# A tuned attention and mixture-of-experts kernel: each PSUM bank of the late stage becomes a tile of its own, the last expert's products change order, and the vector work is listed anew

## The chip, the cores and the metric

The kernel runs on one core of a Trainium2 chip. The metric is the device time of one execution in microseconds (us); the number given for a kernel is the median of its runs. The kernel before took 471.54 us, the median of three runs that lay between 467.0 and 472.02 us.

## The reference

Two stages follow each other. The first is an attention that adds a pooled part (queries, keys and values averaged over four positions) to a local part (a band of seven keys). The second is a mixture of four experts, each with two matrix products, over 1152 tokens:

```python
def _attn_ref(q, k, v):                      # 2 x 8 heads x 576 x 64
    ...
    return out_up + out_local                # pooled + banded softmax attention

def _moe_ref(x, domain_probs, w1, w2):       # N, D, E, F = 1152, 512, 4, 1024
    p = domain_probs / (domain_probs.sum(-1, keepdims=True) + 1e-09)
    out = np.zeros((N, D), dtype=np.float32)
    for e in range(E):
        h = np.maximum(x @ w1[e], 0.0)
        out += p[:, e:e + 1] * (h @ w2[e])
    return out
```

Inputs and output are float32. The kernel splits each float32 operand into a high and a low part (fp32r) and adds three matrix products (low x high, high x low, high x high).

## The kernel before, in words

**Stages.** The first 186 us do the attention and expert 0, interleaved. What the change touches is the late stage: experts 1, 2 and 3, one after the other, each in the same pattern. `late_expert(e)` writes it down as steps with a name, an engine and the steps they depend on; the table `ORDER` at the top of the file is a list of all step names, and the steps are issued in exactly that order, so it sets the order of the instructions on each engine. A layer under the kernel then puts the waits (semaphores) between engines by looking at which tiles an instruction reads and writes.

**Products.** Both matrix products of an expert are done with seven block products in place of eight, a fast matrix multiplication over 2 x 2 blocks. The names of the seven are `1 5 6 2 7 4 3`.

- The first matrix product: for each of four slices i of the hidden features there are seven steps `p<m><e><i>` (line 1034), 12 matmuls each: 6 for the first 288 tokens, then 6 for the other 288. They accumulate in the PSUM areas X, Y, Z. After a product an area is drained into the SBUF tile H by a step `t11 t12 t22 h21` on ACT (lines 1043, 1045) or `h11 h12 h22` on DVE (line 1047). There are seven drains for each i, 28 per expert, 84 in all. Each reads 576 columns: both 288-token halves in one instruction.
- The second matrix product: for each of the seven, two steps `s<m><e><h>` for the token halves h = 0 and 1 (line 1220), 24 matmuls each. Their operands are units of H that ACT rounds (`ah`, lines 1131 and 1135) and DVE subtracts (`ao`, lines 1140 and 1144), and blocks of w2 that ACT rounds (`bh`) and DVE subtracts (`bo`, line 1086). Units live in a ring of three buffers. Sums of H that some units need are `as` (line 1118).
- Two steps `c1` and `c2` (line 1233, 24 matmuls each) do the middle 128 tokens in the area W; their operands are the steps `th to tr ts tdh tdo` (lines 1191 to 1201).
- The results are drained into the accumulator `acc` by steps `d<e><name><h>.<t>` on DVE (line 1242, 256 columns each), by `dw` for the middle tokens (line 1247), and for two of the seven by a scaled copy on ACT (`dt`, line 1267) and an accumulating DMA from POOL's queue (`dd`, line 1270). The next product into the same area has to come after the drain. In the last expert, `st` steps on SP's queue store `acc` to the output as it is finished.

**PSUM.** There are eight banks of 512 float32 columns. In the late stage they are four tiles of two banks, `T["banks"]`, each [128, 2, 512]; X, Y, Z and W are one such tile each, and the roles rotate (`BANKS`). A token half h is one bank of the pair:

```python
T["banks"] = [ps.tile([P, 2, 512], F32, name=f"ps{i}") for i in range(4)]
...
def bank(n, i=None):
    return T["banks"][pair(n, i)]
```

**Order of the second product.** PE issues s1, s5, s2, s6 (two halves each), c1, s7, c2, s4, s3. Into X go 1, 6, 7, 4; into Z go 5 and 3; into Y goes 2. So `s7` waits for the drain of 6 (`x2`), `s4` for the drain of 7 (`x3`), and `s3` for the drain of 5 (`z1`).

**Other queues.** w1 comes over SP's queue (`wl`) and is summed on DVE (`ws`); one slice per expert is built by DMAs alone, copies from SP (`wm`) and accumulating adds from POOL (`wa`). w2 blocks come by `bl<e><m>.<k>`: k = 0 from SP, k > 0 as accumulating DMAs from POOL, through two buffers, one of which is used by product 6 and then by product 4.

Of the kernel before, what the change touches and what calls it, by code (L numbers as in the profile page):

```python
# [15 lines left out]
P = 128  # L16
# [60 lines left out]
    dt1x10 ao151.1 th1 as16.0 dd1x10 s510 ah120.0 as16.1 bh13 ao120.0 s511 ah121.0 bo13 ao121.0 bl17.1 s210 bo16
    ah160.0 wa2020 as17.0 dt1x11 bl14.1 s211 ah161.0 ao160.0 dd1x11 ao161.0 s610 ah170.0 to1 ao170.0 tr1 s611 ts1
    ah171.0 d1x20.0 wa2062 d1x20.1 bh17 ao171.0 c11 bo17 ah140.0 dt1y0 d1x21.0 bl21.0 d1x21.1 bh14 dd1y0 ao140.0 s710
    tdh1 bo14 tdo1 bl26.0 as13.0 s711 ah141.0 wh20 d1x30.0 d1x30.1 c21 ah130.0 ao141.0 d1x31.0 dt1y1 d1x31.1 wo20 s410  # L80
    dd1y1 bl26.1 ao130.0 wl21 s411 d1z10.0 ah131.0 d1z10.1 d1z11.0 ao131.0 d1z11.1 s310 wl22 dw1 d1x40.0 d1x40.1
    d1x41.0 d1x41.1 s311 d1z20.0 d1z20.1 ws21 p120 d1z21.0 bl26.2 d1z21.1 p520 t1120 wh21 p620 wo21 p220 t1220 t2220
    p720 bh21 ws22 wl23 p121 h1120 wh22 h2220 bo21 p521 t1121 bl25.1 p420 t2221 p621 h2120 p320 t1221 p221 wo22 p721
    h1220 h1121 p122 h2221 ws23 ah210.0 p522 t1122 ah211.0 ao210.0 p421 wh23 ao211.0 p622 h2121 t2222 as25.0 p321
    t1222 ah250.0 p222 bh25 wo23 p722 h1221 wl30 h1122 p123 wm304 h2222 wm305 wm306 bo25 p523 t1123 ao250.0 bl22.0
    p422 t2223 p623 h2122 p322 t1223 wa3042 p723 bh26 wa3052 p223 h2223 bh22 h1222 p423 ah210.1 ah211.1 ao210.1 p323
    bo22 h2123 h1123 bl23.0 s120 ao211.1 as25.1 h1223 ah250.1 s121 ah251.0 ao250.1 wa3023 ah251.1 ao251.0 dt2x10
    ao251.1 th2 as26.0 dd2x10 s520 ah220.0 as26.1 bh23 ao220.0 s521 ah221.0 bo23 ao221.0 bl27.1 s220 bo26 ah260.0
    wa3020 as27.0 dt2x11 bl24.1 s221 ah261.0 ao260.0 dd2x11 ao261.0 s620 ah270.0 to2 ao270.0 tr2 s621 ts2 ah271.0
    d2x20.0 wa3062 d2x20.1 bh27 ao271.0 c12 bo27 ah240.0 dt2y0 d2x21.0 bl31.0 d2x21.1 bh24 dd2y0 ao240.0 s720 tdh2  # L90
    bo24 tdo2 bl36.0 as23.0 s721 ah241.0 wh30 d2x30.0 d2x30.1 c22 ah230.0 ao241.0 d2x31.0 dt2y1 d2x31.1 wo30 s420
    dd2y1 bl36.1 ao230.0 wl31 s421 d2z10.0 ah231.0 d2z10.1 d2z11.0 ao231.0 d2z11.1 s320 wl32 dw2 d2x40.0 d2x40.1
    d2x41.0 d2x41.1 s321 d2z20.0 d2z20.1 ws31 p130 d2z21.0 bl36.2 d2z21.1 p530 t1130 wh31 p630 wo31 p230 t1230 t2230
    p730 bh31 ws32 wl33 p131 h1130 wh32 h2230 bo31 p531 t1131 bl35.1 p430 t2231 p631 h2130 p330 t1231 p231 wo32 p731
    h1230 h1131 p132 h2231 ws33 ah310.0 p532 t1132 ah311.0 ao310.0 p431 wh33 ao311.0 p632 h2131 t2232 as35.0 p331
    t1232 ah350.0 p232 bh35 wo33 p732 h1231 h1132 p133 h2232 bo35 p533 t1133 ao350.0 bl32.0 p432 t2233 p633 h2132 p332
    t1233 p733 bh36 p233 h2233 bh32 h1232 p433 ah310.1 ah311.1 ao310.1 p333 bo32 h2133 h1133 bl33.0 s130 ao311.1
    as35.1 h1233 ah350.1 s131 ah351.0 ao350.1 ah351.1 ao351.0 dt3x10 ao351.1 th3 as36.0 dd3x10 s530 ah320.0 as36.1
    bh33 ao320.0 s531 ah321.0 bo33 ao321.0 bl37.1 s230 bo36 ah360.0 ao360.0 bl34.1 dt3x11 as37.0 s231 ah361.0 dd3x11
    ao361.0 s630 ah370.0 to3 ao370.0 tr3 s631 ts3 ah371.0 d3x20.0 bh37 d3x20.1 bo37 dt3y0 c13 ah340.0 ao371.0 dd3y0  # L100
    bh34 d3x21.0 d3x21.1 s730 tdh3 ao340.0 tdo3 bo34 s731 ah341.0 d3x30.0 d3x30.1 as33.0 c23 dt3y1 st5.0 st6.0 ao341.0
# [1277 lines left out]
```

## Time and profile before

| | us |
|---|---|
| median of three runs | 471.54 |
| their range | 467.0 to 472.02 |
| the profiled execution's own time | 471.17 |
| span of its trace, first to last instruction | 469.2 |
| PE (matmul) busy | 449.8, 96% of the span |
| DVE busy | 332.6, 71% |
| ACT busy | 202.8, 43% |
| POOL busy | 105.2, 22% |

The span is 1.97 us shorter than the profiled execution's own time. The page cuts the span into 40 slices of 11.7 us; in all but the last PE is busy for 70% or more. TensorE's granted clock is half of full speed for three slices near the start and full after that (the mean over the span is 0.963), so the late stage runs at full clock. The chain of work that ended last, followed back from the end, is PE for 85% of the span and DVE for 5%; where it leaves PE, PE was waiting.

### The profile page before, as it was taken

The numbers are of one execution on the slowest core, as the hardware profiler recorded it, in microseconds if no ns is written. First come the engines' busy times: TensorE is split into PE (matmuls) and PEld (weight loads), VectorE is DVE, ScalarE is ACT, GpSimd is POOL, SyncE is SP. The second block draws the span as 40 slices with busy tenths as digits, with TensorE's granted clock in tenths as the row PEclk, the third lists the DMA queues.
The fourth block names the chain that finished last, engine by engine and source line by source line (L and its number), as shares of the span: only waits on it lengthen the run. The fifth ranks groups of instructions, "written<-read, shape, count | busy, mean of one in ns | idle before, by whom it ended". The sixth has DMA issues, their size and how long they took to land.

```text
span 469.2 us, 10113 instructions
## 1 busy us (share of the span) xinstructions
PE 449.8 (96%) x4266; PEld 425.1 (91%) x4266; DVE 332.6 (71%) x555; ACT 202.8 (43%) x343; POOL 105.2 (22%) x126
## 2 busy tenths in 40 slices
...
GB/s 181 227 265 106 121 57 85 110 29 32 37 1 46 3 89 28 154 88 133 70 58 113 131 173 85 8 146 57 84 126 120 143 91 1 45 46 121 59 27 177
DMA packets 68941, 43.10 MB, mean 92 GB/s; under 512 B 27616, under 2 KB 66720, under 8 KB 68896
## 3 DMA queue, kind: packets, MB, share of 16 engines
...
## 4 chain that ended last, share of the span: by engine, by line
PE 85%; DVE 5%; POOL 4%; DMA 2%; issue 2%; ACT 1%; SPq 0%; DVEq 0%; POOLq 0%; ACTq 0%
PE ps L1034 29%; PE ps L1220 26%; PE m03h L778 4%; PE m03o L803 3%; POOL wlo L306 3%; PE m02h L778 3%; PE m01h L778 3%; PE m01o L803 2%; PE m02o L803 2%; PE m00o L803 2%; DVE acc L1242 1%; DMA acc<-in_q_dram 1%; PE m00h L778 1%; PE ps L1233 1%; PE wps L232 1%
## 5 line engine op out<-in xcount | busy, mean ns | idle before, releaser
L1220 PE MATMUL ps<-slot,unit 128*128 128x256 f32 x1008 | 121.2, 281 | 6.3 <-DVE acc L1242 6.2
L1220 PEld LDWEIGHTS ps<-slot,unit 128*128 128x128 f32 x1008 | 119.2, 188 | 8.0 <-ACT slot L1199 4.3
L1034 PE MATMUL ps<-xhi,slot 128*128 128x288 f32 x384 | 66.5, 295 | 0.0
L1034 PE MATMUL ps<-xc,slot 128*128 128x288 f32 x432 | 59.8, 295 | 0.0
L1034 PEld LDWEIGHTS ps<-xc,slot 128*128 128x128 f32 x432 | 58.2, 188 | 0.0
L1034 PEld LDWEIGHTS ps<-xhi,slot 128*128 128x128 f32 x384 | 56.3, 188 | 0.1
L1043 ACT ACTIVATE H<-ps 128x576 f32<-128x576 f32 x36 | 23.2, 652 | 52.7 <-PE ps L1034 52.4
L1047 DVE TENSOR_TENSOR H<-H,ps 128x576 f32<-128x576 f32 x36 | 25.5, 747 | 26.8 <-PE ps L1034 26.8
L189 ACT CAST slot<-raw 128x1024 fp32r<-128x1024 f32 (+1 forms) x33 | 41.9, 1279 | 4.5 <-DVE raw L981 4.1
L1080 POOL DMA_DIRECT2D raw<-in_moe_w_dram x15 | 21.0, 1403 | 93.0 <-DMA raw<-in_moe_w_dram 55.2
L1034 PE MATMUL ps<-xlo,slot 128*128 128x288 f32 x192 | 41.1, 295 | 0.0
L987 DVE TENSOR_TENSOR slot<-raw,slot 128x1792 fp32r<-128x1792 f32 x12 | 24.3, 2022 | 21.4 <-PE ps L1034 19.4
L1242 DVE SCALAR_TENSOR_TENSOR acc<-ps,npr,acc 128x256 f32<-128x256 f32 x48 | 20.8, 477 | 25.2 <-PE ps L1220 25.2
L1131 ACT ACTIVATE unit<-H 128x512 fp32r<-128x512 f32 (+1 forms) x24 | 20.0, 844 | 30.5 <-DVE H L1047 17.6
L1118 DVE SCALAR_TENSOR_TENSOR H<-H 128x1024 f32<-128x1024 f32 (+1 forms) x18 | 28.1, 1574 | 5.7 <-ACT H L1045 5.7
L1135 ACT ACTIVATE unit<-H 128x1024 fp32r<-128x1024 f32 x18 | 19.1, 1062 | 29.3 <-PE ps L1220 22.0
L1034 PEld LDWEIGHTS ps<-xlo,slot 128*128 128x128 f32 x192 | 30.7, 188 | 0.0
L1140 DVE SCALAR_TENSOR_TENSOR unit<-H,unit 128x512 fp32r<-128x512 f32 (+1 forms) x24 | 22.7, 953 | 5.4 <-ACT unit L1131 5.3
L1086 DVE TENSOR_TENSOR slot<-raw,slot 128x1024 fp32r<-128x1024 f32 x21 | 25.6, 1217 | 0.0
L306 POOL TENSOR_TENSOR wlo<-raw,whi 128x256 fp32r<-128x256 f32 x28 | 21.2, 791 | 3.3 <-ACT whi L189 3.2
L1144 DVE SCALAR_TENSOR_TENSOR unit<-H,unit 128x1024 fp32r<-128x1024 f32 x18 | 21.7, 1217 | 0.0
L975 POOL DMA_DIRECT2D raw<-in_moe_w_dram x8 | 10.7, 1581 | 42.7 <-ACT H L1043 22.7
...
## 6 DMA issues: line engine op xcount, KB each, us to landing
...
```

Source lines behind the costliest of these rows:

```text
L189: nc.scalar.copy(out_, in_)
L306: eng.tensor_tensor(a[:, us], b[:, us], c[:, us], ALU.subtract)
L778: nc.tensor.matmul(ps[:, :n], w[:, d, cc:cc + P], x[:, d, n0:n0 + n], start=i == 0, stop=i == len(terms) - 1,)
L803: nc.tensor.matmul(ps[:, cs], T[f"{nm}t{f}"][:, hpart, cc:cc + P], w[:, f % 4, cs], start=f == 0 and x == 0, stop=f == KF - 1 and x == 2,)
L987: engine(f"wo{e}{i}").tensor_tensor(w1tile(i, 1), raw1(e, i), f32(w1tile(i, 0)), ALU.subtract)
L1034: nc.tensor.matmul(ps[:, n, :NH // 2], w[:, d * P:(d + 1) * P], x[:, d, n * (NH // 2):(n + 1) * (NH // 2)], start=u == 0 and first_, stop= ...
L1043: nc.scalar.mul(dst, at("Z" if c == "t22" else "X"), -1.0)
L1047: nc.vector.tensor_tensor(dst, dst, at({"h11": "Y", "h12": "Z", "h22": "X"}[c]), ALU.add)
L1086: engine(f"bo{e}{m}").tensor_tensor(w2tile(m, 1), raw2(q), f32(w2tile(m, 0)), ALU.subtract)
L1118: nc.vector.scalar_tensor_tensor(at[o], at[x], 0.0, at[y], ALU.max, op)
L1220: nc.tensor.matmul(ps[:, h, t * 256:t * 256 + 256], a[:, f, t * P:t * P + P], b[:, f], start=first_ and (t, f, x) == (0, 0, 0), stop=(t, f ...
L1242: nc.vector.scalar_tensor_tensor(a, bank(n)[:, h, t * 256:t * 256 + 256], p, a, ALU.mult, ALU.add)
```

## The change

- The four two-bank PSUM tiles of the late stage become eight tiles of one bank. `bank(n, h, i)` gives the bank of token half h.
- The drains `into(i, c)` of the first product become two instructions of 288 columns, one for each half.
- In the last expert the products come in the order 1, 5, 2, 6, 7, 3, 4 (before: 4, then 3). `c2` of that expert comes last of all, and waits for `dw3.0`: the middle tokens are drained and stored in two pieces of 256 columns.
- In the lists of dependencies, the drains into `acc` no longer wait for the earlier drains of the same rows; the stores wait for all of them.
- The table `ORDER` is written anew from the first late expert on. Before it, it is the same. (Line numbers of the changed file are up to 3 higher than those of the profile: line 1242 there is 1244, line 1220 is 1222, line 1233 is 1235.)

```diff
--- before.py
+++ after.py
@@ -70,38 +70,38 @@
...
-    st3.1 ao331.0 st4 d3x40.0 s330 d3x40.1 st0.0 d3x41.0 st7.0 st8.0 st1.0 d3x41.1 st2.0 st3.0 s331 d3z20.0 d3z20.1
-    st5.1 st6.1 d3z21.0 d3z21.1 st7.1 st8.1
...
+    tdo3 st8.1 d3z21.0 s431 d3z20.1 st7.1 d3x40.0 st6.1 d3x40.1 st0.0 d3z20.0 st1.0 st5.1 c23 d3x41.0 d3x41.1 st2.0
+    st3.0 st7.0 st8.0 dw3.1 st4.1
@@ -868,7 +868,7 @@
         T["H"] = pool.tile([P, KF // 2, 2, N], F32, name="H")
         T["s8c"] = late.enter_context(tc.tile_pool(name="s8c", bufs=1, side="right", reuse_waits="tile"))
         ps = late.enter_context(tc.tile_pool(name="ps", bufs=1, space=PSUM, reuse_waits="tile"))
-        T["banks"] = [ps.tile([P, 2, 512], F32, name=f"ps{i}") for i in range(4)]
+        T["banks"] = [ps.tile([P, 512], F32, name=f"ps{i}") for i in range(8)]
 
     def area(i):
 
@@ -942,7 +942,7 @@
     def late_expert(e):
         H = lambda: T["H"]
         A, B_, C, D_, X, F = AREAS[e]
-        SECOND = ("1", "5", "2", "6", "7", "4", "3")
+        SECOND = ("1", "5", "2", "6", "7") + (("4", "3") if e < E - 1 else ("3", "4"))
 
 
         WS = [(A, B_), (C, D_), (X, A), (B_, C)]
@@ -1020,31 +1020,33 @@
 
             return BANKS[e, i]["XZYW".index(n)]
 
-        def bank(n, i=None):
-            return T["banks"][pair(n, i)]
+        def bank(n, h, i=None):
+            return T["banks"][2 * pair(n, i) + h]
 
         def product(m, i):
             k, acc_, first_, _ = PRODUCTS[m]
-            ps = bank(acc_, i)
             hi, lo = tokens[m]()
             wh, wo = w1tile(i, 0)[:, k], w1tile(i, 1)[:, k]
             terms = [(w, x, d) for w, x in ((wo, hi), (wh, hi), (wh, lo)) for d in range(2)]
             for n in range(2):
                 for u, (w, x, d) in enumerate(terms):
                     nc.tensor.matmul(
-                        ps[:, n, :NH // 2], w[:, d * P:(d + 1) * P], x[:, d, n * (NH // 2):(n + 1) * (NH // 2)],
+                        bank(acc_, n, i)[:, :NH // 2], w[:, d * P:(d + 1) * P], x[:, d, n * (NH // 2):(n + 1) * (NH // 2)],
                         start=u == 0 and first_, stop=u == 5, skip_group_check=True,
                     )
 
         def into(i, c):
-            at = lambda n: bank(n, i)[:, :, :NH // 2]
-            dst = H()[:, i, int(c[1]) - 1, (int(c[2]) - 1) * NH:int(c[2]) * NH].rearrange("p (n t) -> p n t", n=2)
-            if c[0] == "t":
-                nc.scalar.mul(dst, at("Z" if c == "t22" else "X"), -1.0)
-            elif c == "h21":
-                nc.scalar.activation(dst, at("X"), AF.Relu)
-            else:
-                nc.vector.tensor_tensor(dst, dst, at({"h11": "Y", "h12": "Z", "h22": "X"}[c]), ALU.add)
+            name = {"t11": "X", "t12": "X", "t22": "Z", "h21": "X", "h11": "Y", "h12": "Z", "h22": "X"}[c]
+            for h in range(2):
+                at = bank(name, h, i)[:, :NH // 2]
+                c0 = (int(c[2]) - 1) * NH + h * (NH // 2)
+                dst = H()[:, i, int(c[1]) - 1, c0:c0 + NH // 2]
+                if c[0] == "t":
+                    nc.scalar.mul(dst, at, -1.0)
+                elif c == "h21":
+                    nc.scalar.activation(dst, at, AF.Relu)
+                else:
+                    nc.vector.tensor_tensor(dst, dst, at, ALU.add)
 
 
         HREAD = {c: list(HUSERS.get(c, [])) for c in ("t11", "t12", "t22", "h21")}
@@ -1211,19 +1213,19 @@
 
         def second(m, h):
             n, first_ = INTO[m]
-            ps = bank(n)
+            ps = bank(n, h)
             fs = (0, 4)
             ah, al, bh, bl = unit(m, h, 0, fs), unit(m, h, 1, fs), w2tile(m, 0), w2tile(m, 1)
             for t in range(2):
                 for f in range(4):
                     for x, (a, b) in enumerate(((al, bh), (ah, bl), (ah, bh))):
                         nc.tensor.matmul(
-                            ps[:, h, t * 256:t * 256 + 256], a[:, f, t * P:t * P + P], b[:, f],
+                            ps[:, t * 256:t * 256 + 256], a[:, f, t * P:t * P + P], b[:, f],
                             start=first_ and (t, f, x) == (0, 0, 0), stop=(t, f, x) == (1, 3, 2), skip_group_check=True,
                         )
 
         def middle(c):
-            w = bank("W")[:, 0, (c - 1) * 256:c * 256]
+            w = bank("W", 0)[:, (c - 1) * 256:c * 256]
             hi, lo = mtile(0), mtile(1)
             pairs = ((1, "1" if c == 1 else "7"), (0, "2" if c == 1 else "3"))
             for r, m in pairs:
@@ -1239,12 +1241,12 @@
             tile_ = (0 if half == "a" else 5) + 2 * h + t
             p = (pr if sign > 0 else npr)[:, tile_, e:e + 1]
             a = acc[:, tile_, c * 256:c * 256 + 256]
-            nc.vector.scalar_tensor_tensor(a, bank(n)[:, h, t * 256:t * 256 + 256], p, a, ALU.mult, ALU.add)
+            nc.vector.scalar_tensor_tensor(a, bank(n, h)[:, t * 256:t * 256 + 256], p, a, ALU.mult, ALU.add)
 
         def gather_mid(c):
             cs = slice(0, 512) if c is None else slice(c * 256, c * 256 + 256)
             a = acc[:, 4, cs]
-            nc.vector.scalar_tensor_tensor(a, bank("W")[:, 0, cs], pr[:, 4, e:e + 1], a, ALU.mult, ALU.add)
+            nc.vector.scalar_tensor_tensor(a, bank("W", 0)[:, cs], pr[:, 4, e:e + 1], a, ALU.mult, ALU.add)
 
         DRAINS = (("x1", "1", "X", "b", 1, 0), ("y", "2", "Y", "b", 1, 0), ("x2", "6", "X", "b", -1, 1),
                   ("x3", "7", "X", "a", -1, 1), ("z1", "5", "Z", "a", -1, 1), ("x4", "4", "X", "a", 1, 0), ("z2", "3", "Z", "b", -1, 1))
@@ -1260,11 +1262,11 @@
                     deps += BUSY.get(pair(n), [])
                 step(f"s{m}{e}{h}", "P", deps, lambda m=m, h=h: second(m, h))
         step(f"c1{e}", "P", [f"to{e}", f"bo{e}1", f"bo{e}2"] + BUSY.get(pair("W"), []), lambda: middle(1))
-        step(f"c2{e}", "P", [f"tdo{e}", f"bo{e}7", f"bo{e}3", f"c1{e}"], lambda: middle(2))
+        step(f"c2{e}", "P", [f"tdo{e}", f"bo{e}7", f"bo{e}3", f"c1{e}"] + ([f"dw{e}.0"] if e == E - 1 else []), lambda: middle(2))
         def scaled_copy(d, n, h):
             t = T[f"part{e}{d}{h}"] = T["parts"].tile([P, 2, 256], F32, tag="part", name=f"part{e}{d}{h}")
             for u in range(2):
-                nc.scalar.mul(t[:, u], bank(n)[:, h, u * 256:u * 256 + 256], pr[:, 5 + 2 * h + u, e:e + 1])
+                nc.scalar.mul(t[:, u], bank(n, h)[:, u * 256:u * 256 + 256], pr[:, 5 + 2 * h + u, e:e + 1])
 
         def added(d, h):
             nc.gpsimd.dma_start(acc[:, 5 + 2 * h:7 + 2 * h, 0:256], T[f"part{e}{d}{h}"], accum_op=ALU.add)
@@ -1282,11 +1284,15 @@
                         DONE[x, c] = [f"dd{e}{d}{h}"]
                     continue
                 for t, x in enumerate(tiles):
-                    step(f"d{e}{d}{h}.{t}", "V", [f"s{m}{e}{h}"] + before[t],
+                    step(f"d{e}{d}{h}.{t}", "V", [f"s{m}{e}{h}"] + [y for y in before[t] if y[0] == "m"],
                          lambda m=m, h=h, t=t, n=n, half=half, sign=sign, c=c: gather(m, h, t, n, half, sign, c))
-                    DONE[x, c] = [f"d{e}{d}{h}.{t}"]
-        step(f"dw{e}", "V", [f"c2{e}"] + DONE.get(4, ["m02.g0"]), lambda: gather_mid(None))
-        DONE[4] = [f"dw{e}"]
+                    DONE[x, c] = before[t] + [f"d{e}{d}{h}.{t}"]
+        if e < E - 1:
+            step(f"dw{e}", "V", [f"c2{e}"] + DONE.get(4, ["m02.g0"]), lambda: gather_mid(None))
+            DONE[4] = [f"dw{e}"]
+        else:
+            for c in range(2):
+                step(f"dw{e}.{c}", "V", [f"c{c + 1}{e}"] + DONE[4], lambda c=c: gather_mid(c))
         for n, d in (("X", "x4"), ("Z", "z2"), ("Y", "y")):
             BUSY[pair(n)] = drained(d, 0) + drained(d, 1)
         BUSY[pair("W")] = [f"dw{e}"]
@@ -1300,11 +1306,8 @@
                 cs = slice(c * 256, c * 256 + 256) if c is not None else slice(0, 512)
                 nc.sync.dma_start(out[t * P:(t + 1) * P, cs], acc[:, t, cs])
             for t in range(NTOK):
-                if t == 4:
-                    step(f"st{t}", "S", [f"dw{e}"], lambda: store(4, None))
-                    continue
                 for c in range(2):
-                    step(f"st{t}.{c}", "S", DONE[t, c], lambda t=t, c=c: store(t, c))
+                    step(f"st{t}.{c}", "S", DONE[t, c] if t != 4 else [f"dw{e}.{c}"], lambda t=t, c=c: store(t, c))
 
     HUSERS, BUSY, DONE = {}, {}, {}
     RAW1, RAW2, PART = [[]], [[], []], [[]]
```

The table moves instructions at two places that the prediction speaks of. The first is DVE in the last expert, around the drains of product 6, which stand on line 1242 here and on line 1244 in the changed file; line 1197 is `ts`, line 1086 is `bo7`, line 1144 is `ao`, line 1140 is `ao4`. A wait in brackets names the engine waited for. Before:

```order
L1197 SCALAR_TENSOR_TENSOR H<-H 128x4x128 [waits Activation_49]
L1242 SCALAR_TENSOR_TENSOR acc<-ps_2541,npr,acc 128x256 [waits PE_49]
L1242 SCALAR_TENSOR_TENSOR acc<-ps_2541,npr,acc 128x256
L1086 TENSOR_TENSOR slot_2502<-raw_2575,slot_2502 128x1024 [waits DMASW0_49,Activation_49]
L1144 SCALAR_TENSOR_TENSOR unit_5021<-H,unit_5021 128x1024
L1242 SCALAR_TENSOR_TENSOR acc<-ps_2541,npr,acc 128x256 x2
L1140 SCALAR_TENSOR_TENSOR unit_5054<-H,unit_5054 128x1024 [waits Activation_49]
L1201 TENSOR_TENSOR slot_2487<-H,slot_2487 128x4x128 [waits Activation_49]
L1086 TENSOR_TENSOR slot_2664<-raw_2593,slot_2664 128x1024 [waits DMASW1_49]
```

All four drains read one tile, ps_2541, and only the first of them waits for PE. In the changed kernel:

```order
L1120 SCALAR_TENSOR_TENSOR H<-H 128x4x512
L1244 SCALAR_TENSOR_TENSOR acc<-ps_2541,npr,acc 128x256 [waits PE_49]
L1244 SCALAR_TENSOR_TENSOR acc<-ps_2541,npr,acc 128x256
L1088 TENSOR_TENSOR slot_2502<-raw_2579,slot_2502 128x1024 [waits DMASW1_49,Activation_49]
L1146 SCALAR_TENSOR_TENSOR unit_5110<-H,unit_5110 128x1024 [waits Activation_49]
L1244 SCALAR_TENSOR_TENSOR acc<-ps_2542,npr,acc 128x256 [waits PE_49]
L1244 SCALAR_TENSOR_TENSOR acc<-ps_2542,npr,acc 128x256
L1146 SCALAR_TENSOR_TENSOR unit_5138<-H,unit_5138 128x1024 [waits Activation_49]
```

The halves are now two tiles, ps_2541 and ps_2542, and each pair of drains has a wait for PE of its own: the first pair no longer comes after the second half's matmuls. The sum for product 3 (line 1118, here 1120) stands ahead of them, and the middle tokens' steps (lines 1197, 1201) have moved behind.

The second place is the end of PE's queue. Each row is one step s or half of a step c. Before, from the second half of c1 on:

```order
L1233 MATMUL ps_2544<-slot_2414,slot_2487 128x256 x12
L1220 MATMUL ps_2541<-slot_2502,unit_4991 128x256 x24
L1220 MATMUL ps_2541<-slot_2502,unit_5021 128x256 x24
L1233 MATMUL ps_2544<-slot_2502,slot_2487 128x256 x12
L1233 MATMUL ps_2544<-slot_2649,slot_2487 128x256 x12
L1220 MATMUL ps_2541<-slot_2664,unit_5054 128x256 x24
L1220 MATMUL ps_2541<-slot_2664,unit_5113 128x256 x24
L1220 MATMUL ps_2542<-slot_2649,unit_5148 128x256 x24
L1220 MATMUL ps_2542<-slot_2649,unit_5207 128x256 x24
```

In the changed kernel:

```order
L1235 MATMUL ps_2547<-slot_2414,slot_2487 128x256 x12
L1222 MATMUL ps_2541<-slot_2502,unit_5079 128x256 x24
L1222 MATMUL ps_2542<-slot_2502,unit_5110 128x256 x24
L1222 MATMUL ps_2543<-slot_2657,unit_5138 128x256 x24
L1222 MATMUL ps_2544<-slot_2657,unit_5200 128x256 x24
L1222 MATMUL ps_2541<-slot_2673,unit_5230 128x256 x24
L1222 MATMUL ps_2542<-slot_2673,unit_5261 128x256 x24
L1235 MATMUL ps_2547<-slot_2502,slot_2487 128x256 x12
L1235 MATMUL ps_2547<-slot_2657,slot_2487 128x256 x12
```

Product 3 (ps_2543 and ps_2544) has moved ahead of product 4 (ps_2541 and ps_2542), so that two products lie between 6, 7 and 4 in the same bank, and c2 has moved from behind product 7 to the very end.

## Rows read from the trace of the kernel before

**Rows 1.** The page: span and engines' busy times over the whole execution.

```profile
span 469.2 us, 10113 instructions
PE 449.8 (96%) x4266; PEld 425.1 (91%) x4266; DVE 332.6 (71%) x555; ACT 202.8 (43%) x343; POOL 105.2 (22%) x126
```

**Rows 2.** Late stage by stretches; columns as in the first row.

```profile
core 0: us, PE busy (x) PEld busy (x) DVE busy (x) ACT busy (x) POOL busy (x), PEclk, DMA share, GB/s
...
253.20:277.65 24.45, 23.14 (x194) 22.56 (x193) 19.89 (x27) 8.83 (x11) 5.00 (x4) 1.00 0.61 130
277.65:322.40 44.75, 44.75 (x340) 44.75 (x339) 27.31 (x37) 21.78 (x28) 4.92 (x4) 1.00 0.39 78
322.40:345.04 22.64, 22.64 (x195) 22.64 (x194) 17.93 (x17) 12.95 (x17) 7.20 (x6) 1.00 0.61 104
345.04:369.55 24.51, 23.22 (x192) 22.64 (x192) 19.89 (x27) 8.84 (x11) 5.00 (x4) 1.00 0.64 138
...
414.10:436.70 22.60, 22.60 (x196) 22.60 (x195) 18.11 (x18) 12.99 (x18) 5.00 (x4) 1.00 0.55 94
436.70:463.85 27.15, 23.47 (x193) 22.69 (x191) 17.95 (x26) 7.20 (x10) 2.39 (x2) 1.00 0.33 88
463.85:469.20 5.35, 0.00 (x0) 0.00 (x0) 1.66 (x4) 0.00 (x0) 0.00 (x0) 0.91 0.30 100
```

**Rows 3.** What PE waited for: total us, times, longest.

```profile
PE ps L1220 <- DVE acc L1242: 6.2, 5, 1.9
```

**Rows 4.** The chain that ended last, end of the last expert: start, us, what.

```profile
437.16 0.47 DVE acc L1242
437.63 1.13 DVE slot L1086
438.76 1.14 DVE unit L1144
439.90 0.80 DVE acc L1242 x2
...
440.83 5.85 PE ps L1220 x48
...
447.59 2.20 DVE H L1118
449.79 1.14 DVE unit L1140
450.92 0.41 DVE acc L1242
```

**Rows 5.** Timeline, last expert: start, us, engine, line, operation, [idle before, releaser].

```profile
436.76 0.88 DVE L1242 SCALAR_TENSOR_TENSOR acc<-ps,npr,acc 128x256 f32<-128x256 f32 x2 [2.06 <-PE ps L1220]
...
463.89 1.66 DVE L1242 SCALAR_TENSOR_TENSOR acc<-ps,npr,acc 128x256 f32<-128x256 f32 x4 [2.86 <-PE ps L1220]
464.40 2.13 SPq L1301 DMA_DIRECT2D out_dram<-acc  x4
```

**Rows 6.** Groups by line: count, busy us, mean ns of one, idle before.

```profile
L1047 DVE TENSOR_TENSOR H<-H,ps 128x576 f32<-128x576 f32 x36 | 25.5, 747 | 26.8 <-PE ps L1034 26.8
L1043 ACT ACTIVATE H<-ps 128x576 f32<-128x576 f32 x36 | 23.2, 652 | 52.7 <-PE ps L1034 52.4
L1131 ACT ACTIVATE unit<-H 128x1024 fp32r<-128x1024 f32 x12 | 12.7, 1062 | 12.9 <-PE ps L1220 12.9
L1242 DVE SCALAR_TENSOR_TENSOR acc<-ps,pr,acc 128x256 f32<-128x256 f32 x12 | 5.0, 476 | 0.0
L1267 ACT ACTIVATE part3x<-ps,pr 128x256 f32<-128x256 f32 x4 | 1.7, 467 | 1.7 <-PE ps L1220 1.7
L1197 DVE SCALAR_TENSOR_TENSOR H<-H 128x512 f32<-128x512 f32 x3 | 2.0, 681 | 0.0
```

**Rows 7.** Timeline, expert 1, first product: a drain and the matmuls behind it.

```profile
203.89 2.08 DVE L1047 TENSOR_TENSOR H<-H,ps 128x576 f32<-128x576 f32 x3
...
204.87 0.69 PE L1034 MATMUL ps<-xhi,slot 128*128 128x288 f32 x4
```

More of the change, by code (lines that the diff above doesn't have):

```diff
@@ L77 @@
[L77 to L101, printed above, removed]
@@ new lines @@
+    ao150.0 bl12.0 p412 t2213 p613 h2112 p312 t1213 wa2052 p713 bh16 h1212 wa2042 p213 h2213 bh12 bo16 p413 ah110.1
+    bo12 bl14.1 ah111.1 p313 h2113 ao110.1 bl13.0 ao111.1 s110 h1113 as15.1 h1213 ah150.1 s111 ah151.0 wa2023 ao150.1
+    ah151.1 ao151.0 dt1x10 ao151.1 th1 as16.0 dd1x10 s510 ah120.0 as16.1 bh13 ao120.0 s511 ah121.0 bo13 ao121.0 bl17.1
+    s210 ah160.0 wa2020 ao160.0 dt1x11 as17.0 s211 ah161.0 dd1x11 ao161.0 s610 ah170.0 to1 ao170.0 tr1 s611 ts1
+    ah171.0 d1x20.0 wa2062 d1x20.1 bh17 ao171.0 c11 dt1y0 bo17 bh14 dd1y0 d1x21.0 bl21.0 ah140.0 d1x21.1 as13.0 s710
@@ new lines @@
+    tdh1 tdo1 ao140.0 s711 ah141.0 d1x30.1 wh20 d1x30.0 ao141.0 c21 ah130.0 bo14 dt1y1 d1x31.1 bl26.0 d1x31.0 dd1y1
+    wo20 s410 ao130.0 wl21 s411 d1z10.0 ah131.0 d1z10.1 d1z11.0 d1z11.1 ao131.0 s310 wl22 d1x40.0 bl26.1 dw1 d1x41.0
+    d1x40.1 d1x41.1 s311 d1z20.1 d1z20.0 ws21 p120 d1z21.1 d1z21.0 p520 t1120 ws22 wh21 p620 wo21 p220 t1220 bl26.2
+    t2220 p720 h1120 wh22 wl23 p121 h2220 bh21 p521 bo21 t1121 bl25.1 p420 t2221 p621 h2120 p320 t1221 p221 wo22 p721
+    h1220 h1121 p122 h2221 ws23 p522 ah210.0 t1122 ao210.0 p421 ah211.0 wh23 ao211.0 p622 h2121 t2222 p321 t1222 p222
@@ new lines @@
+    bh25 wo23 p722 h1221 wm305 wl30 h1122 p123 wm304 h2222 wm306 bo25 p523 t1123 as25.0 bl22.0 p422 t2223 ah250.0 p623
+    h2122 ao250.0 p322 t1223 wa3052 p723 bh26 h1222 wa3042 p223 h2223 bh22 bo26 p423 ah210.1 bo22 bl24.1 ah211.1 p323
+    h2123 ao210.1 bl23.0 ao211.1 s120 h1123 as25.1 h1223 ah250.1 s121 ah251.0 wa3023 ao250.1 ah251.1 ao251.0 dt2x10
+    ao251.1 th2 as26.0 dd2x10 s520 ah220.0 as26.1 bh23 ao220.0 s521 ah221.0 bo23 ao221.0 bl27.1 s220 ah260.0 wa3020
+    ao260.0 dt2x11 as27.0 s221 ah261.0 dd2x11 ao261.0 s620 ah270.0 to2 ao270.0 tr2 s621 ts2 ah271.0 d2x20.0 wa3062
@@ new lines @@
+    d2x20.1 bh27 ao271.0 c12 dt2y0 bo27 bh24 dd2y0 d2x21.0 bl31.0 ah240.0 d2x21.1 as23.0 s720 tdh2 tdo2 ao240.0 s721
+    ah241.0 d2x30.1 wh30 d2x30.0 ao241.0 c22 ah230.0 bo24 dt2y1 d2x31.1 bl36.0 d2x31.0 dd2y1 wo30 s420 ao230.0 wl31
+    s421 d2z10.0 ah231.0 d2z10.1 d2z11.0 d2z11.1 ao231.0 s320 wl32 d2x40.0 bl36.1 dw2 d2x41.0 d2x40.1 d2x41.1 s321
+    d2z20.1 d2z20.0 ws31 p130 d2z21.1 d2z21.0 p530 t1130 ws32 wh31 p630 wo31 p230 t1230 bl36.2 t2230 p730 h1130 wh32
+    wl33 p131 h2230 p531 t1131 bh31 p430 t2231 bo31 p631 h2130 bl35.1 p330 t1231 p231 wo32 p731 h1230 h1131 p132 h2231
```

15 lines of the change are left out of this document (10 added, 5 removed).

## The prediction

> **What bounds the kernel now.** I read the page first: PE is busy for 449.8 of 469.2 us [rows 1]. A change that leaves PE's matmuls as they are can gain only where PE stands still, so the second view is the late stage cut into stretches, all at full clock (1.00) [rows 2]. Each expert has three: the first product (44.75 us in expert 2, PE busy without a gap), the first eight steps of the second product, and its last eight (c1, s7, c2, s4, s3). The two kinds of eight steps are 192 matmuls each and should take the same time. They don't: the clean ones of experts 2 and 3 take 22.64 and 22.60 us, mean 22.62, or 2.83 per step; the last eight take 24.45, 24.51 and 27.15.
>
> The third view says for what PE waits: drains of `acc` on line 1242, 6.2 us in five waits [rows 3]. That is less than the excess of the stretches, since matmuls right after a wait also start more slowly; I use the stretches.
>
> The fourth view, the chain, shows how such a wait comes about. In the last expert it has left PE by 437.16 and runs over DVE through a drain, `bo7`, a unit's `ao` and two more drains until PE resumes with s7 at 440.83 [rows 4]. The first drain started at 436.76, after DVE had sat idle for 2.06 us until PE released it [rows 5]. It drains the half h = 0 of product 6, whose matmuls had ended a step earlier: 436.76 is the end of the other half. So DVE idles first, and then all its work is late at once, while PE has only c1 (2.83 us) to bridge it.
>
> **The change, part by part.**
>
> *One tile per bank.* In the new order the drains of h = 0 have a wait of their own, and can start when s60 ends, one step (2.83 us) sooner. I go through what each later step then waits for, with 0.88 us for two drains [rows 5], 1.14 for a `bo` or an `ao` in a busy queue [rows 4], 1.06 for an `ah` and 0.68 for `ts` [rows 6].
>
> - s7: between the end of s60 and its start lie s61 and c1, 5.66 us. DVE has at most `ts`, two drains, an `ao` and `bo7`: 0.68 + 0.88 + 1.14 + 1.14 = 3.8. It keeps 1.8 us.
> - s4 in experts 1 and 2: between the end of s70 and its start lie s71 and c2, 5.66 us. `ah`, `ao` and then `bo4`, which was moved here, take 1.06 + 1.14 + 1.14 = 3.3, and the drains run beside `ah`. It keeps 2.3 us.
> - s3 in the last expert follows s7 directly: between the end of s61 and its start lie c1, s70 and s71, 8.5 us, against `ao71` and `bo7` (2.28), two drains (0.88), an `ao` (1.14) and four z1 drains (1.66) [rows 5]: 6.0. It keeps 2.5 us. Product 4 then has s71, s30 and s31 to hide behind, and c2, last of all, has s40 and s41 for `tdh` and `tdo`.
>
> Every wait of PE in these stretches so goes, and none of the margins is under 1.5 us. The gain is the excess over a clean stretch: 24.45 - 22.62 = 1.83, 24.51 - 22.62 = 1.89, and 27.15 - 22.62 = 4.53, in the last expert because `as` (2.20), `ao4` (1.14) and a drain stood in DVE's queue between c2 and s4 [rows 4]. Sum 8.25 us. The bounds are 0 (the waits stay) and 8.25 (PE can't be faster than clean).
>
> *The tail.* After the last matmul the span goes on for 5.35 us [rows 2]: four drains, of which the first takes 0.48, and four stores that SP issues from 464.40 on for 2.13 us, 0.53 each [rows 5]; from there to the end, 469.2 - 466.53, it is 2.67. In the change one drain and one store are left behind the last matmul: 0.04 + 0.48 + 0.03 + 0.53 + 2.67 = 3.75 us, a gain of 1.60. Four other stores stand ahead of it on SP, ready about 0.5 us after s41 ends; they take 2.13, so SP is free at 2.65, and the last store is ready at 2.83 + 0.55 = 3.4. It keeps 0.7 us; if that is gone, the gain is between 0 and 1.6. I take 1.60.
>
> *Halved drains of the first product.* 36 instructions on DVE and 48 on ACT become twice as many with half the columns. The trace has no 288-column drain. Lower bound: nothing is lost. Upper bound: each half costs as much as the nearest rows, 256 columns: 476 ns on DVE (line 1242) and 467 on ACT (line 1267), against 747 and 652 for the whole [rows 6]. A pair is then 2 x 0.476 - 0.747 = 0.205 us longer on DVE and 2 x 0.467 - 0.652 = 0.282 on ACT; since 288 is near 256, I take these. Per expert that is 12 x 0.205 = 2.5 and 16 x 0.282 = 4.5 us beside PE's 44.75, where DVE is busy for 27.3 and ACT for 21.8 [rows 2]: 29.8 and 26.3 still fit. What counts is the distance from a drain to the product that reuses its bank. The tightest that I found: a drain starts at 203.89 and ends 0.75 later, at 204.64, and PE is there at 204.87 [rows 7], 0.23 us later. With halves the first bank is free at 204.37, and its product still starts at 204.87; the second is free at about 204.8, and its six matmuls start 6 x 0.133 = 0.8 us later, at 205.67. The distances grow, so I put the cost on the path at 0.
>
> *Moved weight work.* `bo6` goes from the middle of the second product into the end of the first, where DVE has 44.75 - 27.31 = 17 us free; the POOL add `bl4.1`, which waits for it, goes ahead of the `wa` adds and the first `dd` on POOL's queue, which is busy for 5 to 8 us in such a stretch [rows 2]. `bl6.0` waits on SP for the later `bo4`, with the `wl` loads behind it as before. Their covers are a stretch of PE long. If POOL's queue were held up, `dd` and then the next `dt` on ACT would be late. Cost 0.
>
> **Sum.** 8.25 + 1.60 = 9.85 us. The profiled execution took 471.17 (1.97 more than its span), which gives 461.3. The median, 471.54, lies 0.37 above that execution, so for the median I predict 461.7 us.
>
> **Rivals.** About 1%, 4.7 us, is what a measurement of this kernel can tell from no change: its three runs spread over that.
>
> 1. *DVE still sets the pace* (0.14). For it: DVE is busy for 19.89 of the 24.45 us in the closing stretch [rows 2], and would be for 88% of 22.62; in the last expert its work was 17.95 + 1.66. A late `ah` would bring part of the waits back. Against: the margins above. With half of the 8.25 kept and no shorter tail the gain is 4.1: 467.4 us.
>
> 2. *The change doesn't do what it says* (0.07): PE and DVE still exclude each other over both halves, be it by the waits or in PSUM itself. For it: the trace holds no drain that runs beside matmuls into the other bank of its pair. Against: drains run beside matmuls into other pairs throughout the first product, and PE has no gap there [rows 2]. About 471.5 us. [...]
>
> 3. *The halved drains come onto the path* (0.06), the slower side. Place: the 84 drains of the first product and the products behind them. Price: up to 36 x 0.205 + 48 x 0.282 = 20.9 us, if PE waits for the whole of each pair's extra time: 482.6. It cancels the gain from 9.85 / 20.9 = 47% of it on, and the kernel is slower by over 1% from 70%. For it: ACT sat idle before line 1043 for 52.4 us waiting for PE [rows 6], so its drains follow right behind the matmuls. Against: the distances grow, as worked out. [...]
>
> My forecast has the rest, 0.73, from 457 to 464: 457 because the lowest of the runs before, 467.0, less 9.85 is 457.2. Range 457.0 to 467.5: it reaches up to rival 1, with about 0.83 inside. Faster by over 1% (below 466.8): 0.73 and most of rival 1, 0.83. Within 1%: the rest of it and rival 2, 0.11. Slower by over 1%: 0.06.
>
> **What would show it.** Right: the closing stretches take about 22.6 us in all three experts; PE waits for line 1244 no more; the first drain of product 6 starts while s61 runs; from the last matmul to the end it is under 4 us, with one store behind it; the first product still takes 44.5 to 44.8 us per expert, with half drains of 0.4 to 0.5 us. Wrong: a first product longer than 45 us (rival 3), a new wait of PE on an `ao` or a `bo` (rival 1), drains of h = 0 that still start with the end of h = 1 (rival 2), or SP still issuing stores when the last drain is done (the tail).

## The result, and the profile after

The changed kernel takes 456.19 us (median of 4 runs, 455.20 to 456.84) against 470.74 for the kernel before in the same comparison: ratio 0.970, 95% interval 0.964 to 0.976. It is faster, as forecast, but it gained more than the range allowed: 457.0 was its low end. The profiled execution took 456.84 us, its span is 455.1 [rows 1 for before]. Where executions are counted below, two of the 41 later ones of the kernel before are left out as slow, over 1.5% above the fastest of their comparison.

The page: span and the engines' busy times.

```profile
span 455.1 us, 10197 instructions
PE 443.3 (97%) x4266; PEld 420.6 (92%) x4266; DVE 337.8 (74%) x592; ACT 208.3 (46%) x391; POOL 104.7 (23%) x126
```

DVE and ACT are busy for longer than before, PE for 6.5 us less with the same 4266 matmuls (4.2 of them in front of the late stage, where the instructions are the same). The late stage by stretches answers to [rows 2]; columns as in the first row.

```profile
core 0: us, PE busy (x) PEld busy (x) DVE busy (x) ACT busy (x) POOL busy (x), PEclk, DMA share, GB/s
182.28:226.85 44.57, 44.57 (x339) 44.57 (x338) 25.22 (x41) 22.24 (x43) 8.87 (x7) 1.00 0.50 110
...
249.57:272.10 22.53, 22.53 (x194) 22.53 (x194) 19.75 (x29) 8.12 (x9) 4.97 (x4) 1.00 0.68 141
272.10:316.70 44.60, 44.60 (x338) 44.60 (x338) 27.46 (x44) 23.50 (x44) 6.17 (x5) 1.00 0.39 76
316.70:339.32 22.62, 22.62 (x195) 22.62 (x194) 19.61 (x21) 13.76 (x19) 5.81 (x5) 1.00 0.67 108
339.32:361.85 22.53, 22.53 (x194) 22.53 (x194) 19.88 (x29) 8.13 (x10) 4.97 (x4) 1.00 0.66 143
...
428.86:451.61 22.75, 22.73 (x192) 22.53 (x191) 16.76 (x28) 7.78 (x11) 2.39 (x2) 1.00 0.42 114
451.61:455.10 3.49, 0.00 (x0) 0.00 (x0) 0.48 (x1) 0.00 (x0) 0.00 (x0) 1.00 0.27 92
```

The reader is to see that PE's busy time equals the stretch in every row but the last two: the closing stretches take 22.53, 22.53 and 22.75 us (before 24.45, 24.51 and 27.15), and the tail 3.49 (before 5.35). The view of waits has no row for PE in this stage, where [rows 3] had 6.2 us. The chain of the last expert, which left PE for DVE in [rows 4], now stays on PE to the end.

```profile
428.86 2.87 PE ps L1235 x24
431.73 17.01 PE ps L1222 x144
448.74 2.87 PE ps L1235 x24
451.61 0.02 issue
451.63 0.48 DVE acc L1249
```

The timelines of DVE and of PE, around the end of product 6 in the last expert, answer to [rows 5].

```profile
425.59 2.28 DVE L1120 SCALAR_TENSOR_TENSOR H<-H 128x2048 f32<-128x2048 f32 x1
427.79 0.87 DVE L1244 SCALAR_TENSOR_TENSOR acc<-ps,npr,acc 128x256 f32<-128x256 f32 x2
```

```profile
425.78 3.08 PE L1222 MATMUL ps<-slot,unit 128*128 128x256 f32 x25
428.69 3.03 PE L1235 MATMUL ps<-slot,slot 128*128 128x256 f32 x24
```

The drain of half h = 0 starts at 427.79, while PE still computes h = 1 into the next bank (until 428.86). Before, it started with the end of h = 1, after DVE had stood idle for 2.06 us [rows 5].

The halves of the first product's drains, in the groups by line, answer to [rows 6] (lines 1043, 1047 and 1034 there are 1045, 1049 and 1033 here).

```profile
L1049 DVE TENSOR_TENSOR H<-H,ps 128x288 f32<-128x288 f32 x72 | 29.3, 449 | 19.6 <-PE ps L1033 19.6
L1045 ACT ACTIVATE H<-ps 128x288 f32<-128x288 f32 x72 | 27.8, 411 | 50.1 <-PE ps L1033 50.0
```

So the late stage is 10.5 us shorter: 283.3 us before, from the first matmul of the first expert at 185.93 to the end, and 272.8 now, from 182.28. The other 3.6 of the 14.1 us between the two spans lie in front of it, where the two kernels have the same instructions.

### The profile page after: what moved, and what is told of

It is laid out like the page before. It is cut to its first block, busy times and chain, and to the rows that moved or that the text cites. A ratio compares the mean times of both kernels' runs of the same rounds, so it can differ in the third digit from the quotient of the medians.

```text
span 455.1 us, 10197 instructions
## 1 busy us (share of the span) xinstructions
PE 443.3 (97%) x4266; PEld 420.6 (92%) x4266; DVE 337.8 (74%) x592; ACT 208.3 (46%) x391; POOL 104.7 (23%) x126
## 3 DMA queue, kind: packets, MB, share of 16 engines
HBM read 36.69 MB, written 2.36 MB: 86 GB/s over the span
## 4 chain that ended last, share of the span: by engine, by line
PE 87%; POOL 4%; DMA 4%; DVE 2%; SPq 1%; issue 1%; ACT 1%; POOLq 0%; ACTq 0%
PE ps L1033 29%; PE ps L1222 26%; PE ps L1235 4%; PE m03h L778 4%; PE m03o L803 4%; POOL wlo L306 3%; PE m02h L778 3%; PE m01h L778 3%; PE m01o L803 3%; PE m02o L803 2%; PE m00o L803 2%; PE m00h L778 1%; DMA acc<-in_q_dram 1%; DMA vw<-in_v_dram 1%; DMA q0n<-in_q_dram 1%; SPq L276 1%
## 5 line engine op out<-in xcount | busy, mean ns | idle before, releaser
L1222 PE MATMUL ps<-slot,unit 128*128 128x256 f32 x1008 | 119.7, 280 | 0.0
L1045 ACT ACTIVATE H<-ps 128x288 f32<-128x288 f32 x72 | 27.8, 411 | 50.1 <-PE ps L1033 50.0
L1049 DVE TENSOR_TENSOR H<-H,ps 128x288 f32<-128x288 f32 x72 | 29.3, 449 | 19.6 <-PE ps L1033 19.6
L1146 DVE SCALAR_TENSOR_TENSOR unit<-H,unit 128x1024 fp32r<-128x1024 f32 x18 | 22.0, 1222 | 8.1 <-ACT unit L1137 8.0
```

Of the source, the lines that this page charges most:

```text
L1045: nc.scalar.mul(dst, at, -1.0)
L1049: nc.vector.tensor_tensor(dst, dst, at, ALU.add)
L1222: nc.tensor.matmul(ps[:, t * 256:t * 256 + 256], a[:, f, t * P:t * P + P], b[:, f], start=first_ and (t, f, x) == (0, 0, 0), stop=(t, f, x ...
```

## The experiments

Medians of few executions carry the chance of the early part (shown with e5 and e6), so the experiments on the late stage are compared by it: the time from the start of the first expert's first product to the end, 283.3 us before and 272.8 in the change.

**One-bank tiles and halved drains alone, old order (e1).** Against the kernel before (the drains as in e3's diff):

```diff
-        T["banks"] = [ps.tile([P, 2, 512], F32, name=f"ps{i}") for i in range(4)]
+        T["banks"] = [ps.tile([P, 512], F32, name=f"ps{i}") for i in range(8)]
...
-        def bank(n, i=None):
-            return T["banks"][pair(n, i)]
+        def bank(n, h, i=None):
+            return T["banks"][2 * pair(n, i) + h]
```

> The kernel before with one tile per PSUM bank and the halved drains of the first product, its old order of work and its old last expert kept. Theory 1 (what makes PE wait is that a drain of half h = 0 is held until the matmuls of h = 1 end): the waits of PE on line 1242's drains go without any new order, the closing eight steps take about 22.6 us in all three experts, the tail stays at 5.3 us with four stores in it, so the span from the start of the first expert's first product is some 8.3 us shorter than before (283.4 to about 275.1). Rival (the new order of DVE's work and of the last products is what removes the waits): closing stretches of 24.5, 24.5 and 27.2 us as before, nothing gained. On the early part (185.8 us before, 182.2 in the changed kernel, with the same instructions): if it is a matter of chance at which time the granted clock rises, it lies anywhere between 182 and 186; if the tiles make the difference, it is 182.

457.90 us, ratio 0.976 (0.972 to 0.981). Its closing stretches and its tail:

```profile
248.84:271.38 22.54, 22.54 (x195) 22.54 (x194) 19.80 (x29) 8.84 (x11) 5.00 (x4) 1.00 0.65 141
338.60:361.13 22.53, 22.53 (x194) 22.53 (x194) 19.79 (x29) 8.85 (x11) 5.00 (x4) 1.00 0.66 144
428.13:450.84 22.71, 22.69 (x193) 22.49 (x191) 17.41 (x26) 6.56 (x9) 2.38 (x2) 1.00 0.43 117
450.84:454.80 3.96, 0.00 (x0) 0.00 (x0) 0.88 (x2) 0.00 (x0) 0.00 (x0) 1.00 0.20 67
```

Theory 1 holds, and by more than expected: every wait goes without the new order, and the tail shrinks too, to 3.96 us instead of staying at 5.3, since two of the last product's four drains are done before its last matmul. The late stage takes 454.8 - 181.56 = 273.2 us: the tiles, with the halved drains that they need, are worth 10.1 of the 10.5.

**The new order alone, two-bank tiles (e2).** Against the changed kernel:

```diff
-        T["banks"] = [ps.tile([P, 512], F32, name=f"ps{i}") for i in range(8)]
+        T["banks"] = [ps.tile([P, 2, 512], F32, name=f"ps{i}") for i in range(4)]
...
-            return T["banks"][2 * pair(n, i) + h]
+            return T["banks"][pair(n, i)][:, h]
```

> The changed kernel with the eight banks again as four tiles of two banks, everything else of the change kept (order of work, last expert's products, one store behind the last matmul). Theory 1: the waits of PE are back, about 1.2 us or more at s7 and at s4 in each expert, so that the closing stretches take 24 to 27 us; only the tail is as short as in the change (3.5 us, gain 1.8): against the kernel before a gain of 0 to 3 us, against the changed kernel a loss of 7 to 10. Rival (the order does it): closing stretches of 22.6 us, time of the changed kernel. Early part: 182 if the order is what shortens it, 186 if the tiles are, anywhere between by chance.

465.62 us, ratio 0.992 (0.989 to 0.995); late stage 465.1 - 184.29 = 280.8 us, 2.5 less than before, 8.0 more than the change. The tail is 4.35 us, not the 3.5 expected. Its closing stretches, PE's waits, and the chain ahead of s4 in expert 1:

```profile
251.59:277.06 25.47, 23.06 (x194) 22.68 (x194) 19.87 (x27) 8.11 (x9) 4.75 (x4) 1.00 0.56 124
344.30:369.75 25.45, 23.03 (x194) 22.66 (x194) 19.88 (x27) 8.12 (x9) 3.68 (x3) 1.00 0.57 124
436.75:460.75 24.00, 23.01 (x192) 22.61 (x191) 17.65 (x30) 7.78 (x11) 2.39 (x2) 1.00 0.36 94
```

```profile
PE ps L1222 <- DVE acc L1244: 5.8, 5, 1.3
```

```profile
263.62 1.14 DVE slot L1088
264.76 0.80 DVE acc L1244 x2
...
265.60 11.46 PE ps L1222 x96
```

Five waits are back. Experts 1 and 2 have two each: the one at s7 is as long as before (1.27 us in expert 1), and one of 1.14 us at s4 is new there, for a `bo4` of 1.14 us now stands in DVE's queue ahead of the drains that s4 waits for. So their closing stretches are longer than before. The last expert has one wait, 0.97 us between the halves of product 7. Only the last expert gains from the order.

**Halved drains alone (e3).** The two-bank tiles of before, with one drain per half:

```diff
+            for h in range(2):
+                at = bank(name, i)[:, h, :NH // 2]
```

> The kernel before with the drains of the first product in two halves each and nothing else changed: the two-bank tiles stay, so the halves free nothing sooner and only their price is left. Prediction on record: half drains of 0.41 to 0.48 us, the first product still 44.8 us per expert, total as before within 1%. Rival (the halved drains come onto the path): the first products grow, up to 4 us per expert at 0.2 us per pair of DVE and 0.16 per pair of ACT, 470.7 to 480. A first product that is shorter than before would show that the halves help by themselves.

467.74 us, ratio 0.998 (0.995 to 1.001); late stage 465.3 - 181.76 = 283.5 us. A first product and a closing stretch of it:

```profile
273.70:318.31 44.61, 44.61 (x339) 44.61 (x338) 27.88 (x48) 22.64 (x44) 4.92 (x4) 1.00 0.39 79
340.95:365.58 24.63, 23.34 (x194) 22.76 (x194) 19.89 (x27) 8.84 (x11) 5.00 (x4) 1.00 0.65 139
```

As predicted: the halves cost nothing in PE's time and give nothing either.

**The last expert in the old order (e4).** The changed kernel with product 4 before product 3 and c2 behind product 7 there, and the table's rows for that expert written for this order:

```diff
-        SECOND = ("1", "5", "2", "6", "7") + (("4", "3") if e < E - 1 else ("3", "4"))
+        SECOND = ("1", "5", "2", "6", "7") + ("4", "3")
```

> The changed kernel with the last expert's products in the old order (product 4 before product 3, c2 right behind product 7, the four stores of product 3 last). Theory A (one-bank tiles alone end the waits of the last expert, the order of its products only shortens the tail): no wait of PE in the last closing stretch, 22.6 us, tail of 5.3 us instead of 3.5, so 1.6 to 1.9 us slower than the changed kernel. Theory B (as the prediction counted it, part of the 4.53 us came from the long DVE work between c2 and s4, and the new order removes it): a wait of 0.5 to 2.6 us at s4 too, 2.3 to 4.5 us slower.

456.24 us, ratio 0.973 (0.969 to 0.976); late stage 453.5 - 180.22 = 273.3 us.

```profile
426.80:449.50 22.70, 22.68 (x192) 22.48 (x191) 16.65 (x26) 6.56 (x9) 2.39 (x2) 1.00 0.42 112
449.50:453.50 4.00, 0.00 (x0) 0.00 (x0) 0.88 (x2) 0.00 (x0) 0.00 (x0) 0.87 0.28 94
```

No wait, so theory B falls. Theory A's mechanism holds and its size doesn't: the new order of the last products is worth 4.00 - 3.49 = 0.5 us, not 1.6 to 1.9.

**Both kernels once more (e5, e6).** No edit.

> The changed kernel once more, in more executions, beside the kernel before. Theory A (the early part's 3.6 us between the two profiles is chance: the granted clock falls to 1.2 GHz for a stretch of 10 to 34 us whose start differs from one execution to the next): the spans of either kernel spread over 4 to 6 us, the longer the lower the mean granted clock, and at equal mean clock the changed kernel is 10 to 11 us shorter. Rival (the change itself shortens the early part): the changed kernel never shows a mean clock below 0.975, and at equal clock the difference is 12 to 14 us.

> The kernel before once more, for another profile of its early part. Theory A (chance): the stretch at 1.2 GHz differs in length from the 34 us of the first profile, the first product of the first expert starts sooner or later with it (by the profiles so far 180.2 to 185.9 us), and the part behind that start takes 283.3 us again. Rival (its early part is always the slow one): 34 us at 1.2 GHz and a start at 185.9 again.

The changed kernel gave 455.82 to 460.67 us, ratio 0.979 (0.974 to 0.983). Its profiled execution was a long one this time (span 458.9), and that of the kernel before a shorter one (465.7). PE and its granted clock: the first profile of the kernel before, that of the changed kernel, then e5 and e6.

```profile
10.00:20.00 10.00, 9.84 (x130) 0.54 0.92 251
...
40.00:50.00 10.00, 9.89 (x206) 0.75 0.21 48
```

```profile
10.00:20.00 10.00, 9.13 (x143) 0.83 0.90 239
...
```

```profile
10.00:20.00 10.00, 9.84 (x129) 0.53 0.90 234
...
40.00:50.00 10.00, 9.80 (x206) 0.76 0.43 120
```

```profile
10.00:20.00 10.00, 9.04 (x141) 0.84 0.92 240
20.00:30.00 10.00, 10.00 (x182) 0.50 1.08 227
30.00:40.00 10.00, 9.89 (x116) 0.64 0.90 255
40.00:50.00 10.00, 8.84 (x229) 1.00 0.69 142
```

The third column from the right is the clock, 0.50 being half of full speed. No view gives a frequency; the 1.2 GHz of the expectations is this 0.50, and an estimate from the changed kernel's chain gives a like rate: at full clock 336 matmuls of 288 columns (line 1033) take 44.57 us, 132.6 ns each, and 72 of 512 (`m03o`, line 803) 16.38 us, 227.5 ns each, so 224 columns more take 94.9 ns, 2.36 columns per ns, which is 1.18 at half the clock. Before's first profile and the changed kernel's second one both run at 0.50 for some 34 us (9.2 + 20 + 5 and 9.4 + 20 + 4.8); before's second profile does so for some 20 (3.2 + 10 + 7.2), falling when the changed kernel's first one does (0.84 and 0.83 in the row from 10 to 20 us). Cut at the start of the first expert, e5 and then e6 show:

```profile
0.00:186.08 186.08, 177.98 (x2108) 155.22 (x2109) 141.56 (x319) 75.22 (x177) 59.54 (x89) 0.91 0.36 88
186.08:458.90 272.82, 269.31 (x2161) 269.11 (x2159) 195.90 (x273) 133.04 (x214) 45.18 (x37) 1.00 0.49 98
```

```profile
0.00:182.54 182.54, 174.17 (x2108) 151.76 (x2109) 142.12 (x319) 75.38 (x177) 59.40 (x89) 0.94 0.38 89
182.54:465.70 283.16, 271.63 (x2161) 269.70 (x2159) 191.01 (x236) 127.49 (x166) 45.56 (x37) 1.00 0.46 95
```

The late stage repeats to 0.2 us in either kernel; the early part is 182.3 and 186.1 us in the one, 185.9 and 182.5 in the other. Theory A holds and both rivals fall: the changed kernel shows mean clocks down to 0.962, and the kernel before starts its first expert 3.4 us sooner in its second profile. The spread of the kernel before is wider than the 4 to 6 us of the theory. Over e1, e5 and e9's comparisons, 39 executions of it have spans of 460.7 to 470.4 us (mean 466.0 at a mean clock of 0.976) and ten of the changed kernel 453.4 to 458.9 (mean 455.5 at 0.977): at equal clock the change is worth 10.5 us, what the late stages differ by.

**A known lateness on DVE (e8).** The changed kernel with 16 memsets in each expert ahead of the first drain of product 6:

```diff
+        def lag():
+            for _ in range(16):
+                nc.vector.memset(T["lz"], 0.0)
+        step(f"lag{e}", "V", [f"to{e}"], lag)
```

> The changed kernel with 16 short memsets on DVE, 2.6 to 3.6 us in all, in each expert ahead of the drain of half h = 0 of product 6: a known lateness against the margin of 1.8 us that the prediction gives s7. Theory (the margin is what the prediction says): PE waits at s7 for the lag less 1.8, 0.8 to 1.8 us in each expert, 2.4 to 5.4 us in all. Rival 1 (no margin, DVE sets the pace): the whole lag, 7.8 to 10.8 us. Rival 2 (far more margin): nothing.

463.03 us; late stage 278.3, 5.5 more than the change. DVE's timeline in expert 1, PE's waits, and that closing stretch:

```profile
247.93 4.04 DVE L1299 MEMSET lz<- 128x128 f32 x16
251.89 0.75 DVE L1245 SCALAR_TENSOR_TENSOR acc<-ps,npr,acc 128x256 f32<-128x256 f32 x2
```

```profile
PE ps L1223 <- DVE slot L1089: 3.5, 3, 1.4
PE ps L1223 <- DVE acc L1245: 1.0, 1, 1.0
```

```profile
250.60:274.79 24.19, 22.79 (x194) 22.59 (x194) 22.72 (x38) 8.12 (x9) 4.97 (x4) 1.00 0.57 131
```

The lag was 4.04 us (2.6 to 3.6 expected) and cost 24.19 - 22.53 = 1.66 here: the margin of s7 is 2.4 us where I had reckoned 1.8. PE waits for a slot that DVE writes (`bo7`), as the prediction's sum for s7 has it; in the last expert it waits for a drain first. In the change DVE is not the bound yet: it is busy for 19.75 of the 22.53 us. With the lag it is busy for 22.72, more than PE's 22.53.

**PE's early gaps filled (e7, e10, e9).** Since the clock falls early, I added small matmuls on zeros to PE's early idle time: 27 at five places in e7 and e10, the first 12 alone in e9.

```diff
-WARM = [14, 0, 0, 0, 0, 0, 0, 0, 0, 0, ..., 1, 3, 0, 0, 14, 6, 6, 3, 3, 6]
+WARM = [14, 3, 0, 0, 0, 0, 0, 3, 0, 6, ..., 1, 15, 0, 3, 14, 6, 6, 3, 3, 6]
```

> The changed kernel with 27 more of the small matmuls on zeros in PE's early gaps (12 ahead of the wait at 7 to 9 us, 15 at four places between 22 and 28 us); the late part is untouched. Theory (PE's idle time ahead of the fall is what lets the granted clock fall): the stretch at 1.2 GHz comes later or not at all, the first product of the first expert starts at 178 to 181 us, and the median is 1 to 3 us under the changed kernel's. Rival (where the clock falls is not set by these gaps, or the added matmuls delay the work behind them): 27 x 0.09 to 0.18 = 2.4 to 4.9 us of added PE work, of which some lies in gaps: 0 to 3 us slower.

> The kernel with all 27 added matmuls once more, for a second profile, since the one at hand (span 452.6) is its fastest execution and the other six took 3.7 to 5.8 us more. Theory: the first product of the first expert starts 3 to 5 us later than the 179.84 of that profile, and the rest behind it takes 272.8 us as before; the place of the loss in the early part is what is looked for. Rival: the early part is as in that profile and the loss lies in the late part.

> The changed kernel with only the first 12 of the added small matmuls, those ahead of PE's wait at 7 to 9 us; after that wait the clock fell at 10.8 to 10.9 us in the two profiles with the longest stretch at 1.2 GHz (34 us). Theory A (this idle time lets the clock fall early, and the 15 later matmuls are what made the kernel with all 27 no faster): no run with a mean clock under 0.97 any more, median 1 to 2 us under the changed kernel's 456.4. Theory B (PE's matmuls in that place delay the work behind them as much as the clock gives back): median 456 to 459, spread as in the changed kernel.

e7 took 458.24 us (454.41 to 460.25) at mean clocks of 0.976 to 0.992, e9 457.38 (456.99 to 458.22) at 0.969 to 0.985, and e10's one execution 458.37. Neither is shorter than the 456.44 of the changed kernel over its ten runs (0.962 to 0.989). In e7 the clock is higher, 0.984 on the mean against 0.977; in e9 it is not. e7's profiled execution was its fastest, and its first expert starts at 179.84 us, as the theory had it; e10's early part and its clock:

```profile
0.00:183.70 183.70, 174.72 (x2162) 152.06 (x2163) 141.56 (x319) 75.26 (x177) 60.39 (x89) 0.96 0.38 89
183.70:456.50 272.80, 269.31 (x2161) 269.11 (x2159) 195.86 (x273) 133.06 (x214) 45.19 (x37) 1.00 0.49 98
```

The loss is in the early part, 183.70 us at a clock of 0.96, where the changed kernel's first profile had 182.28 at 0.94. The theory falls for the time; the runs don't show at which of the added places the work behind was delayed. e9 has neither a long execution nor a short one, which in six executions can be chance. Neither version beats the change.

## Why the prediction was wrong

**The step that failed** is the one from the sum to the time: "The median, 471.54, lies 0.37 above that execution, so for the median I predict 461.7", and with it the low end, "the lowest of the runs before, 467.0, less 9.85 is 457.2". Both take the three runs shown for where the kernel before lies. e5 and e6 put another reading in place of that: its early part is chance by 4 us, with the length of a stretch at half clock, and the profiled execution was one with a long stretch. Of the 39 further executions, one is as long as 471.54; their median is 467.75, and the lowest 462.67. From 467.75 the same gain of 9.85 gives 457.9, inside the range, and the measured gain of 10.5 gives 457.3. Some 0.2 us more lie outside the span (471.17 - 469.2 = 1.97 before, 456.84 - 455.1 = 1.74 now). The rest, 0.9 us down to 456.19, fits chance on the other side: the result's four executions have mean clocks of 0.977 to 0.984, so none has the long stretch. The six of e5, three of them at 0.962 to 0.966, have a median of 458.08, inside the range. So a miss by 0.8 us was bad luck in part; the base was too high all the same. By the means of all 39 and all ten, 467.96 and 457.31, the change is worth 10.65. The profile of before had it in view: the page's row of the clock shows the stretch, and I cut the windows only from the late stage on.

**The sum of 9.85** came out as 10.45, every term with its sign. Closing stretches: 1.83, 1.89 and 4.53 forecast. Cut where the chains of before have the end of the last matmul (277.81 and 369.73; my windows ended at 277.65 and 369.55), those of before are 24.59, 24.69 and 27.12, which gives 2.06, 2.16 and 4.37 us. (The 44.75 us of the first product in [rows 2] has 0.16 too much for the same reason.) The slower start after a wait, which the prediction gives as the reason why the waits, 6.2 us, are less than the 8.25, is there but small: in the trace of before the first matmul after each of the five waits takes 355 to 387 ns, where 280 is usual, and the next starts 192 to 225 ns behind it, where 117 is usual, 0.4 us in all. Tail: 1.60 forecast, 5.35 - 3.49 = 1.86 measured; the term mis-sized there is the issue of the last store, 0.33 us where 0.53 was taken.

**What each part does** I had not separated. I named the moved `bo4` and the new last products as reasons why s4 and s3 keep their margins, and the tail as theirs alone. e1 and e4 show that the tiles by themselves end all waits and bring 1.4 of the tail's 1.86; the order of the last products brings 0.5 (e4), and without the tiles (e2) the new order makes experts 1 and 2 slower.

**Halved drains at nothing**: right, by e3 and by the rows: the first products take 44.57 and 44.60 us. A half takes 449 ns on DVE and 411 on ACT, so a pair is 0.151 and 0.170 us longer than the whole, 36 x 0.151 + 48 x 0.170 = 13.6 us in all that PE does not wait for. Rival 3 with its price was real work, in the wrong place to matter. The forecast's upper bounds for a pair were 0.205 and 0.282 us, taken from rows of 256 columns.

**Rival 1** (DVE sets the pace) falls by e8's margin of 2.4 us; **rival 2** by the drain that starts at 427.79 beside matmuls into the other bank; **rival 3** by e3.
